# Top-k attention into a PReLU feed-forward: one Exp for two duos, scores copied two slots ahead, new slot orders, and the factor 1 - alpha moved from the output weights to the Relu

## The chip, the cores and the metric

The kernel runs on one core of a Trainium2 chip. The metric is the device time of one execution in microseconds. The core's engines each work through their own queue in order: TensorE (PE; its weight loads are shown as PEld), VectorE (DVE), ScalarE (ACT), GpSimd (POOL) and SyncE (SP, which here only issues DMAs).

## The reference

```python
# q, k, v: (8, 8, 576, 64); w_in (512, 2048); w_out (2048, 512); alpha (2048)
scores = q @ k.T / 8                                   # per batch and head
kth = np.partition(scores, -32, axis=-1)[..., -32:-31] # 32nd largest of each row
scores = np.where(scores >= kth, scores, -1e9)
attn = softmax(scores)
x = (attn @ v).transpose(0, 2, 1, 3).reshape(4608, 512)
h = x @ w_in
g = np.maximum(h, 0.0) + alpha * np.minimum(h, 0.0)
out = g @ w_out                                        # (4608, 512) float32
```

The kernel uses g = (1 - alpha) * relu(h) + alpha * h. The second term is linear in x, so w_in * alpha @ w_out is worked out once (tiles `w_lin_b`), and each output tile is the sum of x @ w_lin and of relu(h) with the factor 1 - alpha, times w_out.

## The kernel before

**Duos and slots.** The 8 x 8 x 576 score rows are cut into 144 "duos": two blocks of 128 query rows with 576 scores each (`duos`; 18 of a batch; "n" duos are the same rows of two heads, "m" duos collect the 64-row tails of heads). A software pipeline runs over slots n = 0 to 143, and a drain written out by hand follows. A duo d passes through these steps:

- `st_qk` (PE): scores into the one PSUM tile `ps_sc`, in slot d - 1; `st_exit` (ACT): one copy of 1,152 columns to an SBUF tile `s_sb`, at the end of slot d - 1. There are six `s_sb` tiles.
- the search, in slot d (DVE, in `dve_slot`): twelve MAX8 over groups of 96 scores into `up` and `small`. In odd slots the results of two duos go through `threshold_steps`: `fold` (two compares `bot` and `small`, four MAX8), `negate`, `least` (four MAX8) and `turn`, which writes the threshold into tile `p`.
- `st_count` in slot d + 2 (ACT): two Sign instructions with accumulator against that threshold into `sg`; `st_y` (POOL): two products `y`; `row` (DVE): one MAX8 over each `y`, into `p`.
- `pick_steps` (DVE) in even slots: three small instructions that give the exact 32nd value in `KZ`.
- `st_exp` (ACT) and `st_cut` (ACT, POOL) in slot d + 4: Exp of the duo's 1,152 scores into `w`, two Sign instructions against the exact threshold into `f`, the product `w` times `f` on POOL, then a DMA transpose (SP) to `wT`.
- `st_av` (PE) in slot d + 7 or d + 8, `norm_a` and `norm_b` (DVE) in even slots for two duos, then a DMA transpose to `xT`.

**Feed-forward.** When a chunk of `xT` is complete, `mlp_ready` queues hidden units (`h_pe`: matmuls into PSUM tile `ph`), Relus (`h_relu`, to `gT`) and output parts (`o_pe`: matmuls into `pz`; `o_act`: copy; `o_sp`: store). Slots take one or two of each; where nothing is ready `keep_warm` issues matmuls on the tile `idle`. `h_relu` is a DVE `tensor_scalar` with max, or on request an ACT Relu; the drain requests ACT ten times.

**Weights.** In slots 2 to 15 `w_out` comes as fp32 (`w_st`, POOL's queue), and `scale_out` makes two bf16 tiles of each of its 16 blocks: on ACT `w_out_b` = w_out * (1 - alpha), and on DVE `w_la` = w_out * alpha, of which the linear part is made.

**Order.** Every instruction goes through the class `Ordered`, so that each engine runs in the order of the program text; all of them therefore carry line 32 in the profile, and groups are told apart by tile names. The order inside a slot is the order of the statements in the loop `for n in range(ND)`. For ACT it is count, o_act, exp, cut, exit, copies of `qkT`; for DVE search, (fold,) Relu, (negate,) row 0, (least, turn,) norm, row 1, norm.

Of the kernel before, what the change touches and what calls it, by code (L numbers as in the profile page):

```python
# [17 lines left out]
NG = 6  # L18

# [40 lines left out]
def fast_path(tc, q, k, v, moe_w_in, moe_w_out, moe_alpha, out, flag):  # L60
# [16 lines left out]
    duos = []  # L77
# [15 lines left out]
    with ExitStack() as ctx:  # L93
# [5 lines left out]
        s_p = pool("s", 6)  # L99
# [47 lines left out]
        def sm(ins, reads, writes):  # L147
# [8 lines left out]
            DVE.small.add(ins.ins.name)  # L156
            recent.append((ins.ins, reads, writes))
            del recent[:-60]
# [10 lines left out]
        ws = [const.tile([128, 2, 640], BF16, name=f"w_{i}") for i in range(4)]  # L169
# [3 lines left out]
        alpha1m = const.tile([128, NFT], FP32, name="alpha1m")  # L173
        w_lin_b = [const.tile([128, DMODEL], BF16, name=f"w_lin_b{i}") for i in range(4)]
# [6 lines left out]
        for t in ws:  # L181
            POOL.memset(t[:, :, S:640], 0.0)
# [77 lines left out]
        def st_exit(n):  # L260
            s = s_p.tile([128, 2, S], FP32, name="s_sb", tag="s")
# [55 lines left out]
        def dve_slot(n, f_late):  # L317

            norm = norm_of(n)
            rows = duos_at("count", n)  # L320
# [15 lines left out]
            turn = None  # L336
            if n % 2:
                fold, negate, least, turn = threshold_steps(n // 2)
                fold()
                if n < ND - 1:  # L340
                    h_relu()
                negate()
            else:
                h_relu()
            for d in rows:
                row(d, 0)
            if turn:
                least()
                turn()
            if norm:  # L350
                norm_a(norm)
            for d in rows:
                row(d, 1)
            if norm:
                norm_b(norm)
            if f_late:
                h_pe()
                h_relu()
# [6 lines left out]
        for d in range(ND):  # L365
            for kind, lag in (("count", 2), ("cut", 4), ("exp", 4), ("av", 8 if d < 13 else 7)):
# [3 lines left out]
        for d in range(1, ND, 2):  # L370
            stage["norm", d + (8 if d < 13 else 7)] = d

        def st_count(n, rows=(0, 1)):
            s, p9 = T["s", n], T["p9", n // 2]
            if rows[0] == 0:
                T["sg", n] = two.tile([128, 2, S], BF16, name="sg", tag="sg", bufs=3)
                if n % 2 == 0:
                    T["cs", n // 2] = three.tile([128, 4], FP32, name="cs", tag="cs")
            sg, cs = T["sg", n], T["cs", n // 2]
            for i in rows:  # L380
                r = 2 * (n % 2) + i
                ACT.activation(sg[:, i, :], s[:, i, :], AF.Sign, bias=p9[:, r, 0:1], scale=-1.0,
                               accum_out=cs[:, r:r + 1])

        def st_y(n):
            y = two.tile([128, 2, S], FP32, name="y", tag="y")
            sg = T.pop(("sg", n))
            for i in range(2):
                POOL.tensor_tensor(y[:, i, :], T["s", n][:, i, :], sg[:, i, :], ALU.mult)
            T["y", n] = y  # L390
# [4 lines left out]
        def st_cut(n):  # L395
            w, s = ws[n % 4][:, :, 0:S], T.pop(("s", n))
            f = two.tile([128, 2, S], mybir.dt.uint8, name="f", tag="sg", bufs=3)
            for i in range(2):
                ACT.activation(f[:, i, :], s[:, i, :], AF.Sign, bias=KT[:, 2 * n + i:2 * n + i + 1])
            POOL.tensor_tensor(w, w, f.bitcast(mybir.dt.float8e4), ALU.mult)  # L400
# [162 lines left out]
        def h_relu(eng=None):  # L563
            if act:
                ch, f0, e_n, ph = act.pop(0)
                if eng is ACT:
                    ACT.activation(ch["g"][:, f0:f0 + e_n, :], ph, AF.Relu)
                else:
                    DVE.tensor_scalar(ch["g"][:, f0:f0 + e_n, :], ph, 0.0, None, ALU.max)
# [36 lines left out]
        for b in range(1, B):  # L606
            for i in range(KPB):
                p = KPB * b + i
                s0 = NB * (b - 1) + 4 + 4 * i + (2 if p == NPAIR - 2 else 0)
# [25 lines left out]

        def scale_out(f):
            if f % 8 == 0:
                hold["wl", f // 8] = gp.tile([128, 8, 512], BF16, name="w_la", tag="gT")
            src = hold["st", f // 4][:, f % 4, :]
            ACT.activation(w_out_b[f // 4][:, f % 4, :], src, AF.Copy, scale=alpha1m[:, f:f + 1])  # L640

            sm(DVE.tensor_tensor(hold["wl", f // 8][:, f % 8, :], src,
                                 alpha_ps[:, f:f + 1].to_broadcast([128, 512]), ALU.mult),
               [(304 + f, 305 + f)], [])
# [91 lines left out]
        for n in range(ND):  # L736
            now[0] = n
            run(n, "kd")
            o_sp()

            if n > 4 and not h_pe():
                keep_warm()
            wide_copy = n % 2 and (n, "prep") in todo
            if n > 3:
                run(n, "prep", 1)
            if n and on(n + 1):
                st_qk(n + 1)
            if n < 4:
                run(n, "prep", 2)
            if 0 < n < 5:  # L750
                keep_warm()
            for m in duos_at("av", n):
                st_av(m)
            late = len(hq) > (9 if n < 118 else 4 if n < 132 else 3) and n % 2 == 0 and not (on(n + 1) and duos[n + 1][0] == "m")

            for m in duos_at("count", n):
                st_count(m)
                st_y(m)
            if ready() > 4 or not wide_copy:
                o_act()  # L760
            for m in duos_at("exp", n):
                st_exp(m)
            if not norm_of(n):
                run(n, "ld")
            run(n, "lin_out")
            did = o_pe()
            run(n, "w")

            dve_slot(n, late)
            for m in duos_at("cut", n):  # L770
                st_cut(m)
            if n and on(n + 1):
                st_exit(n + 1)
            run(n, "cast")
            if (n, "lin") in todo:
                run(n, "lin")
            elif not ready() > (2 if n < 128 else 1) or on(n + 2) and duos[n + 2][0] == "m" or not o_pe():
                if n and not did:
                    keep_warm()
            while pend:  # L780
                short = len(pend[0][0].shape) == 3
                wide = pend[0][0].shape[1] == 512
                on_dve = n > 3 and (short and n > 16 or wide and (n < 17 or n % 2 == 0))
                prep_evac(DVE.tensor_copy if on_dve else ACT.copy)
            if n == 1:
                sm(DVE.tensor_copy(alpha_ps, aps), [], [(304, 320)])
                ACT.activation(alpha1m, aps, AF.Copy, scale=-1.0, bias=1.0)
            run(n, "scale")
            if norm_of(n):
                st_xT(norm_of(n) - 1)  # L790
                st_xT(norm_of(n))
                run(n, "ld")
# [42 lines left out]
        o_sp()  # L835
        st_av(D - 6)
        h_pe(2)
        h_relu(ACT)
        h_pe(2)
        h_relu(ACT)  # L840
        o_act()
        o_sp()
# [361 lines left out]
```

## Time and profile before

| | |
|---|---|
| median of 3 runs | 814.86 us (814.15 to 816.9) |
| profiled execution | 814.44 us, of which the span of the trace is 812.4 us |
| busy in the span | PE 734.3, DVE 755.8, ACT 767.0, POOL 713.6 us |
| mean granted TensorE clock | 0.994 |
| moved by DMA | 99.90 MB |

The span is the time from the first instruction to the last in the trace; 2.04 us of the profiled execution lie outside it. Busy time counts the union of an engine's instructions. On ACT and DVE the recorded instructions of one queue overlap at their ends, so the step from one start to the next is shorter than the recorded duration.

### The profile page before, as it was taken

How to read it: one execution, taken by the hardware profiler on the slowest of the kernel's cores; microseconds unless marked ns; L12 is line 12 of the kernel's file. 1: busy time of each engine (PE TensorE's matmuls, PEld its weight loads, DVE VectorE, ACT ScalarE, POOL GpSimd, SP SyncE). 2: the span in 40 equal slices, each digit the busy share in tenths (PEclk: the TensorE clock that was granted, in tenths of full speed). 3: DMA queues.
4: the chain of work that ended last, by engine and by line, in shares of the span. 5: the costliest groups of instructions: out<-in, count | busy, mean ns of one | idle time of the engine just before them, and what ended most of it. 6: DMA issues, size and time to landing. Idle time of an engine off the chain costs nothing.

```text
span 812.4 us, 17847 instructions
## 1 busy us (share of the span) xinstructions
PE 734.3 (90%) x5375; PEld 421.4 (52%) x5448; DVE 755.8 (93%) x3470; ACT 767.0 (94%) x1265; POOL 713.6 (88%) x565
## 2 busy tenths in 40 slices
PE   8888899989989998889989989898989999999886
PEld 5333455545545555555545555454545555556563
DVE  4999999999999999999999999999999999999961
ACT  5999999999999999999999999999999999999971
POOL 2898899999999999989999999999999988998860
PEclk9999999999999999999999999999999999999999
DMA  7799976665565575655576555665566565544361
GB/s 153 196 176 173 178 145 133 115 118 116 124 121 122 113 124 120 127 122 105 127 140 117 129 110 124 108 123 117 119 136 116 116 134 100 99 99 89 82 114 37
DMA packets 342327, 99.90 MB, mean 123 GB/s; under 512 B 336128, under 2 KB 336400, under 8 KB 342224
## 3 DMA queue, kind: packets, MB, share of 16 engines
q1 hardware_dynamic: 338928, 91.18, 58.0%
q0 software_dynamic: 1952, 7.09, 3.7%
q8 instruction: 45, 0.74, 0.4%
q10 hardware_dynamic: 1344, 0.43, 0.2%
q14 instruction: 58, 0.48, 0.2%
HBM read 36.71 MB, written 9.44 MB: 57 GB/s over the span
## 4 chain that ended last, share of the span: by engine, by line
DVE 33%; PE 22%; ACT 18%; POOL 12%; issue 10%; SPq 2%; DMA 2%; ACTq 0%; POOLq 0%; DVEq 0%
DVE small L32 11%; PE ps_sc L32 7%; DVE p L32 7%; POOL y L32 7%; DVE up L32 6%; PE pz L32 5%; ACT f L32 5%; ACT sg L32 4%; ACT s_sb L32 4%; POOL w L32 4%; PE ph L32 4%; DVE gT L32 4%; PE xo L32 3%; ACT w L32 3%; SPq L32 2%
## 5 line engine op out<-in xcount | busy, mean ns | idle before, releaser
L32 POOL TENSOR_TENSOR y<-s_sb,sg 128x576 f32<-128x576 f32 x288 | 362.2, 1279 | 25.2 <-ACT sg L32 24.5
L32 POOL TENSOR_TENSOR w<-w,f 128x1152 bf16<-128x1152 bf16 x142 | 317.8, 2238 | 45.8 <-ACT f L32 44.1
L32 ACT ACTIVATE sg<-s_sb,p 128x576 bf16<-128x576 f32 x288 | 221.6, 774 | 10.6 <-DVE p L32 8.3
L32 DVE MAX8 up<-s_sb 128x8 f32<-128x96 f32 x864 | 212.1, 245 | 11.0 <-ACT s_sb L32 10.9
L32 DVE MAX8 p<-y 128x8 f32<-128x576 f32 x288 | 215.0, 748 | 7.3 <-POOL y L32 6.4
L32 DVE MAX8 small<-s_sb 128x8 f32<-128x96 f32 x864 | 216.2, 250 | 0.0
L32 ACT ACTIVATE f<-s_sb,KZ 128x576 uint8<-128x576 f32 x284 | 203.8, 769 | 0.0
L32 PE MATMUL ps_sc<-qkT 64*128 64x512 f32 (+2 forms) x768 | 183.0, 566 | 22.9 <-ACT s_sb L32 22.5
L32 ACT ACTIVATE w<-s_sb 128x1152 bf16<-128x1152 f32 x144 | 166.9, 1159 | 0.0
L32 ACT COPY s_sb<-ps_sc 128x1152 f32<-128x1152 f32 x144 | 159.2, 1106 | 5.8 <-PE ps_sc L32 5.6
L32 PE MATMUL ph<-xT,w_in_b 128*128 128x256 bf16 (+1 forms) x1472 | 149.6, 249 | 7.0 <-DMA xT<-x 3.1
L32 PE MATMUL pz<-w_out_b,gT 128*128 128x512 bf16 x545 | 142.1, 379 | 9.4 <-issue 6.0
L32 PEld LDWEIGHTS <-w_in_b 128*128 128x128 bf16 x1472 | 119.6, 98 | 50.2 <-issue 10.0
L32 PE MATMUL xo<-v,wT 128*128 128x65 bf16 (+3 forms) x1600 | 126.1, 198 | 0.6 <-DVE x L32 0.6
L32 PEld LDWEIGHTS <-wT 128*128 128x128 bf16 (+3 forms) x1600 | 97.3, 99 | 28.9 <-issue 0.8
L32 DVE TENSOR_SCALAR gT<-ph 128x512 bf16<-128x512 f32 x134 | 90.4, 674 | 8.6 <-PE ph L32 8.6
L32 PEld LDWEIGHTS ps_sc<-qkT 64*128 64x128 f32 (+1 forms) x768 | 55.5, 169 | 66.8 <-ACT s_sb L32 35.0
L32 PEld LDWEIGHTS ps_sc<-kd,qkT 128*128 128x128 f32 x256 | 38.1, 188 | 97.1 <-issue 93.3
L32 PEld LDWEIGHTS <-gT 128*128 128x128 bf16 x576 | 54.6, 98 | 59.1 <-DVE gT L32 4.7
L32 PE MATMUL ps_sc<-kd,qkT 128*128 128x128 f32 x256 | 62.5, 326 | 0.0
L32 PE MATMUL rest<-idle 128*128 128x512 bf16 x200 | 52.5, 389 | 6.6 <-DVE gT L32 4.4
L32 ACT ACTIVATION_READ_ACCUMULATOR sg<-s_sb,p 128x1 f32 x288 | 56.2, 195 | 0.0
(67 smaller groups left out, 569.5 us busy)
## 6 DMA issues: line engine op xcount, KB each, us to landing
k_st<-in_k_dram SPq DMA_DIRECT2D x64, 128.0 KB, 2.8
v_st<-in_v_dram SPq DMA_DIRECT2D x64, 128.0 KB, 2.9
q_st<-in_q_dram SPq DMA_DIRECT2D x62, 128.0 KB, 2.7
out_dram<-o_sb SPq DMA_DIRECT2D x29, 256.0 KB, 2.5
w_st<-in_moe_w_out_dram POOLq DMA_DIRECT2D x4, 1024.0 KB, 7.3
wT<-w SPq DMA_TRANSPOSE x143, 3.5
w_in_b<-in_moe_w_in_dram POOLq DMA_DIRECT2D x4, 512.0 KB, 6.6
k_st<-in_k_dram SPq DMA_DIRECT2D x32, 32.0 KB, 2.6
```

Source lines behind the costliest of these rows:

```text
L32: ins = self.tc.keep_in_program_order(f(*a, **kw))
```

## The change

- One Exp instruction (`exp_two`) handles two duos (2,304 columns) from slot 17 on, at the end of every odd slot, behind the Signs. For that the six score tiles become one tile `s_all` and the four `w` tiles become two.
- From slot 8 on `st_qk` and `st_exit` work on duo n + 2 instead of n + 1.
- The statements of a slot become named steps, run in the order of a string; one string each for even and odd slots, before slot 18 and from it on. Each Sign and each half of `st_y` and `st_cut` has its own step. In odd slots the threshold steps `least` and `turn` come behind row 1, `fold` behind the Relu.
- The drain's order is a string too. All Relus are on DVE; the last pairs of Exps in the drain are two instead of four.
- `h_relu` computes max(h, 0) * (1 - alpha) with one `scalar_tensor_tensor`, whose second input is `alpha1m` broadcast along the tokens. `w_out_b` is loaded as bf16 by four DMAs on POOL's queue in slots 17, 19, 21 and 22; ACT's 16 products in `scale_out` go. DVE's 16 stay.
- Of the wide `qkT` copies of slots 4 to 17 those in odd slots go from DVE to ACT. The loads of `q` and of `v` are issued one slot later and one slot earlier, in most cases.

```diff
+LEAD = 8
+EV = "DADADADADADADADADA"
+SC = "DDDDDDDDDDDDDDDD"
+MODE = 18
+PAIRS = 18
+HEAD_E = "kd osp h prep qk av c0 c1 oact exp ld ope S R r0 na r1 nb late k0 k1 exit cast ope2 evac xt"
+HEAD_O = "kd osp h prep qk av c0 c1 oact exp ld ope S F R N r0 L T na r1 nb late E k0 k1 exit cast ope2 evac xt"
+EVEN = "kd osp h prep av c0 c1 oact ld qk ope S evac R r0 na r1 nb late k0 k1 exit cast ope2 xt"
+ODD = "kd osp h prep av qk ope c0 c1 oact ld S R F r0 N r1 L T late k0 k1 E evac exit cast ope2 xt"
+DRAIN = "osp a6 h RD h RD oact osp c1 p1 n6 RD c0 k3 r10 now op a5 op h op r11 RD h a4 r00 r01 k2 p0 n4 e1 RD oact osp h op e0 RD m1 m0 w2 op op oact osp h RD h RD tw a3 td h RD a1 a0 na nb h RD a2 n2 x0 ..."
...
+        wp = [const.tile([128, 4, 640], BF16, name=f"w_{i}") for i in range(2)]
+        ws = [wp[i // 2][:, 2 * (i % 2):2 * (i % 2) + 2, :] for i in range(4)]
+        s_all = const.tile([128, 12, S], FP32, name="s_sb")
...
         def st_exit(n):
-            s = s_p.tile([128, 2, S], FP32, name="s_sb", tag="s")
+            s = s_all[:, 2 * (n % 6):2 * (n % 6) + 2, :]
             ACT.copy(s, two_of(T.pop(("ps", n)), 960, S))
...
+        def exp_two(n):
+            c = 2 * (n % 6)
+            ACT.activation(wp[n // 2 % 2][:, :, 0:S], s_all[:, c:c + 4, :], AF.Exp, scale=att_scale)
...
-        def h_relu(eng=None):
+        def h_relu():
             if act:
                 ch, f0, e_n, ph = act.pop(0)
-                if eng is ACT:
-                    ACT.activation(ch["g"][:, f0:f0 + e_n, :], ph, AF.Relu)
-                else:
-                    DVE.tensor_scalar(ch["g"][:, f0:f0 + e_n, :], ph, 0.0, None, ALU.max)
+                DVE.scalar_tensor_tensor(out=ch["g"][:, f0:f0 + e_n, :], in0=ph, scalar=0.0,
+                                         in1=alpha1m[:, f0:f0 + e_n].unsqueeze(2).to_broadcast(list(ph.shape)),
+                                         op0=ALU.max, op1=ALU.mult)
...
-                at(s0 - 2, "ld", lambda p=p: load_one(p, "q"))
+                at(s0 - (2 if b == 1 else 1), "ld", lambda p=p: load_one(p, "q"))
-                at(s0 + 6 - early, "ld", lambda p=p: load_one(p, "v"))
+                at(s0 + (6 if b == 1 and i < 2 else 5) - early, "ld", lambda p=p: load_one(p, "v"))
...
+        def w_out_load(i):
+            POOL.dma_start(w_out_b[i], moe_w_out[512 * i:512 * i + 512, :].rearrange("(f p) n -> p f n", p=128))
...
-            ACT.activation(w_out_b[f // 4][:, f % 4, :], src, AF.Copy, scale=alpha1m[:, f:f + 1])
...
+            at((17, 19, 21, 22)[i], "w", lambda i=i: w_out_load(i))
...
+        def ahead(n):
+            return [m for m in ([n + 1] if n < LEAD else [n + 1, n + 2] if n == LEAD else [n + 2]) if n and on(m)]
...
+            def t_E():
+                if n % 2 and n >= PAIRS - 1 and on(n - 3):
+                    exp_two(n - 3)
```

In the strings S is the search, R the Relu, F, N, L, T are fold, negate, least and turn, r0 and r1 the rows, c0 and c1 a Sign of `st_count` with its `y`, k0 and k1 a Sign of `st_cut` (the product behind k1), na and nb the norm, evac the `qkT` copies; in the drain RD is a Relu, m a mask, e an Exp, a an `st_av`, and the digit counts back from the last duo.

More of the change, by code (lines that the diff above doesn't have):

```diff
@@ L734, in fast_path, with evac @@
         PE.transpose(aps, a16, ident_f[0:NFT, 0:NFT])
[L736 to L779, printed above, removed]
+        def ahead(n):
+            return [m for m in ([n + 1] if n < LEAD else [n + 1, n + 2] if n == LEAD else [n + 2]) if n and on(m)]
+        def evac(n):
             while pend:
@@ L794, in picked, with is_late @@
+        def is_late(n):
+            return len(hq) > (9 if n < 118 else 4 if n < 132 else 3) and n % 2 == 0 and not (on(n + 1) and duos[n + 1][0] == "m")
+        for n in range(ND):
+            slot(n)
         def picked(m):
```

316 lines of the change are left out of this document (175 added, 141 removed).

## The prediction

> **What bounds the kernel now.** First I cut the span into the stages by the table of busy time by window (window, its length, busy us of PE, PEld, DVE, ACT and POOL with instruction counts, clock, DMA share, GB/s).
>
> ```profile
> 0.00:20.00 20.00, 17.82 (x91) 11.45 (x92) 9.02 (x61) 11.69 (x24) 4.66 (x28) 1.00 0.73 155
> 20.00:120.00 100.00, 86.60 (x500) 40.97 (x502) 94.46 (x425) 98.43 (x168) 92.35 (x79) 0.97 0.93 176
> 120.00:760.00 640.00, 588.67 (x4358) 341.56 (x4422) 624.61 (x2897) 628.34 (x1028) 593.13 (x442) 1.00 0.59 118
> 760.00:812.40 52.40, 41.19 (x429) 27.46 (x436) 27.75 (x90) 28.51 (x49) 23.49 (x18) 0.97 0.39 74
> ```
>
> In the long middle stage ACT idles 11.7 us of 640 and DVE 15.4: two engines are full, POOL (46.9 idle) and PE (51.3) follow. In the weight stage (20 to 120) ACT alone is full (1.6 idle; DVE 5.5). In the drain none is. So a gain must take work or waiting off both ACT and DVE in the middle, off ACT in the weight stage. Next, what the idle time waits for, in the list of waits of the middle stage (us, times, longest), and the groups of POOL and of DVE's rows there:
>
> ```profile
> POOL w L32 <- ACT f L32: 39.0, 63, 1.1
> ACT sg L32 <- DVE p L32: 7.7, 20, 1.7
> DVE up L32 <- ACT s_sb L32: 5.5, 19, 0.4
> ACT s_sb L32 <- PE ps_sc L32: 1.5, 2, 1.3
> DVE p L32 <- POOL y L32: 1.4, 4, 0.4
> L32 POOL TENSOR_TENSOR y<-s_sb,sg 128x576 f32<-128x576 f32 x243 | 305.7, 1279 | 6.6 <-ACT sg L32 6.4
> L32 POOL TENSOR_TENSOR w<-w,f 128x1152 bf16<-128x1152 bf16 x121 | 270.9, 2239 | 40.3 <-ACT f L32 39.0 <-DVE p L32 1.0
> L32 POOL CAST v<-v_st 128x256 bf16<-128x256 f32 x52 | 20.8, 399 | 0.0
> L32 DVE MAX8 p<-y 128x8 f32<-128x576 f32 x242 | 180.8, 747 | 1.9 <-POOL y L32 1.4
> ```
>
> The two full engines wait for each other: DVE for the score copy (5.5), ACT for the threshold (7.7). 243 products y are 121.5 slots, so a slot takes 640 / 121.5 = 5.27 us and a pair of slots 10.53; the stage has 61 pairs.
>
> **One Exp for two duos.** Busy time misleads here, because ACT's records overlap. The timeline (start, duration) gives the true steps:
>
> ```profile
> 402.17 1.15 ACT L32 ACTIVATE w<-s_sb 128x1152 bf16<-128x1152 f32 x1
> 403.22 1.43 ACT L32 ACTIVATE f<-s_sb,KZ 128x576 uint8<-128x576 f32 x2
> 404.56 1.10 ACT L32 COPY s_sb<-ps_sc 128x1152 f32<-128x1152 f32 x1
> 405.55 0.78 ACT L32 ACTIVATE sg<-s_sb,p 128x576 bf16<-128x576 f32 x1
> ```
>
> An Exp occupies ACT for 403.22 - 402.17 = 1.05 us. No Exp of 2,304 columns is in the trace; I bound it by how ACT's time grows with columns:
>
> ```profile
> L32 ACT ACTIVATE f<-s_sb,KZ 128x576 uint8<-128x576 f32 x284 | 203.8, 769 | 0.0
> L32 ACT ACTIVATE w<-s_sb 128x1152 bf16<-128x1152 f32 x144 | 166.9, 1159 | 0.0
> L32 ACT COPY s_sb<-ps_sc 128x1152 f32<-128x1152 f32 x144 | 159.2, 1106 | 5.8 <-PE ps_sc L32 5.6
> L32 ACT COPY o_sb<-pz 128x512 f32<-128x512 f32 x35 | 19.8, 567 | 7.5 <-PE ph L32 6.3 <-PE pz L32 1.2
> ```
>
> From Sign to Exp it is (1159 - 769) / 576 = 0.68 ns a column, so 1,152 more columns cost 0.78 us and a pair saves 1.05 - 0.78 = 0.27. But the Sign reads a bias tile and the Exp does not; the two copies are of one kind and give (1106 - 567) / 640 = 0.84 ns, 0.97 us, and a saving of 0.08. No saving is the other end. I take 0.09: 61 x 0.09 = 5.5 us off ACT in the middle, ends 0 and 16.5. The Trainium skill (ScalarE: Activation LUTs, What ACT_TABLE_LOAD costs) says that each instruction with a tile as bias pays about 93 ns more and that neighbours overlap by as much; by it the wide Exp saves an estimated 93 ns a pair, against the 0.27 that the first reading of the rows offers.
>
> **Lead of two slots.** The copy that search n + 2 needs ends a whole slot, some 5 us, ahead, so the 5.5 us of DVE up <- ACT s_sb go. The qk matmuls still wait for the copy before, as now, in a PE with 51 us idle. The copy overwrites the tile of the duo whose Signs stand just ahead of it on ACT, and adds no wait. Next late for DVE is y.
>
> **New slot order.** DVE's timeline shows a stall inside its busy time:
>
> ```profile
> 407.30 0.24 DVE L32 MAX8 up<-s_sb 128x8 f32<-128x96 f32 x1
> 407.46 0.25 DVE L32 MAX8 small<-s_sb 128x8 f32<-128x96 f32 x1
> 407.74 0.25 DVE L32 TENSOR_TENSOR bot<-up,small 128x96 f32<-128x96 f32 x1
> ```
>
> Neighbouring MAX8 start 0.16 apart; bot starts 0.28 behind the one whose result it reads. With the Relu between them that 0.12 goes: 61 x 0.12 = 7.3 us. The threshold's last steps now stand behind row 1, so ACT's first Sign of an even slot gets it some 0.67 us later in DVE's order; that is priced among the rivals. Moving Exp behind the Signs of the cut lets POOL's product start a step of 1.05 earlier: part of its 39 us of waiting goes, on an engine that is not full.
>
> **Middle stage.** DVE sheds 5.5 + 7.3 = 12.8 us. ACT sheds 5.5 + 1.5 = 7.0 and can shed more only from its 7.7 us of waiting for the threshold, which arrives sooner when DVE no longer waits. The stage shrinks by something between 7.0 and 12.8; I take 10. Then ACT has 628.3 - 5.5 = 622.8 of 630, 98.9%, as full as now, which is why I don't take more. The ends are 0 (each wait is replaced by another) and 17 (ACT never idle).
>
> **The Relu with the factor.** The rows that bound its price:
>
> ```profile
> L32 DVE TENSOR_SCALAR gT<-ph 128x512 bf16<-128x512 f32 x134 | 90.4, 674 | 8.6 <-PE ph L32 8.6
> L32 DVE TENSOR_SCALAR neg<-small 128x128 f32<-128x128 f32 x72 | 20.2, 281 | 0.4
> L32 DVE TENSOR_TENSOR w_la<-w_st,small 128x512 bf16<-128x512 f32 x16 | 10.5, 675 | 0.0
> L32 DVE TENSOR_TENSOR small<-small,cs 128x36 f32<-128x36 f32 x72 | 13.3, 184 | 0.0
> L32 DVE SCALAR_TENSOR_TENSOR pk<-small,p 128x36 f32<-128x36 f32 x72 | 12.9, 179 | 0.1
> L32 DVE SCALAR_TENSOR_TENSOR w<-s_sb,KZ,w 128x576 bf16<-128x576 f32 x4 | 4.8, 1262 | 0.0
> L32 ACT ACTIVATE gT<-ph 128x512 bf16<-128x512 f32 x10 | 5.8, 593 | 7.1 <-PE ph L32 7.1
> ```
>
> The new form reads one input from PSUM (ph) and one from SBUF. The two-input w_la does so too, on as many columns, in 675 ns, one more than the Relu's 674; pk has the very operation, with operands placed alike, and takes no longer than the plain product of its size (179 to 184). The dear end is the mask, 1,262 for 576, but both its inputs are in SBUF; at its rate 512 columns are 1,122 ns. I take 675: nothing. The Trainium skill speaks against the change here: VectorE: DVE Perf Modes (The perf-mode tier table) grants an instruction with one tensor input up to twice the rate on PSUM, and one with two inputs never. It would cost if the old Relu ran at a doubled rate; by the rows it doesn't, (674 - 281) / 384 = 1.02 ns a column, hardly different from w_la's.
>
> **Weight stage.** ACT loses its products, DVE one wide copy.
>
> ```profile
> L32 ACT ACTIVATE w_out_b<-w_st,alpha1m 128x512 bf16<-128x512 f32 x16 | 11.4, 742 | 0.0
> 37.41 1.34 ACT L32 ACTIVATE w_out_b<-w_st,alpha1m 128x512 bf16<-128x512 f32 x2
> 38.65 0.77 ACT L32 ACTIVATE sg<-s_sb,p 128x576 bf16<-128x576 f32 x1
> w_st<-in_moe_w_out_dram POOLq DMA_DIRECT2D x4, 1024.0 KB, 7.3
> L32 POOL DMA_DIRECT2D w_st<-in_moe_w_out_dram x4 | 3.3, 818 | 0.0
> ```
>
> Two take 1.24 us, so 16 take 9.9. DVE, with 5.5 us idle, becomes the bound: I take 4 us, ends 0 and 5.5. The four bf16 loads cost POOL 4 x 0.82 = 3.3 us around slots 17 to 22, hidden by its idle time (about 0.4 us a slot, so several slots long), and land in 7.3 us, about a slot and a half; the output parts begin at slot 24. If that cover is gone it is 3.3 us. The q loads pass the DMA transposes of an even slot's end only to stand behind the next slot's short issues, in the place of v's, which moved the other way: nothing.
>
> **Drain.** Its chain runs over the masks:
>
> ```profile
> 771.03 1.06 ACT L32 ACTIVATE gT<-ph 128x512 bf16<-128x512 f32 x2
> 771.99 0.77 ACT L32 ACTIVATE sg<-s_sb,p 128x576 bf16<-128x576 f32 x1
> 773.64 4.99 POOL L32 TENSOR_TENSOR y<-s_sb,sg 128x576 f32<-128x576 f32 x4
> 781.01 4.82 DVE L32 SCALAR_TENSOR_TENSOR w<-s_sb,KZ,w 128x576 bf16<-128x576 f32 x4
> ```
>
> Two Relus (0.96 us of ACT) no longer stand ahead of the last Signs, but POOL starts the y's only at 773.64, 0.9 behind the end of the first Sign (771.99 + 0.77), so it is POOL that is late there and little is won. Two Relus now stand on DVE between the last rows and the masks: 2 x 0.67 = 1.35 us later. The other Relus find DVE idle (24.6 us of this stage), and the pair of Exps that left the drain costs nothing there. I take +0.7, ends -1 and +2.
>
> **The sum.** 812.4 - 10 - 4 + 0.7 = 799.1 us of span; with the 2.04 us outside it 801.1. The profiled execution (814.44) lies 0.42 under the median of the runs, so the median should be **801.5 us**.
>
> **The rivals.**
>
> *The waits change places.* The two engines stay as loosely full as now, because the threshold comes later in DVE's order and ACT's 7.7 us of waiting for it grow by what DVE stops losing. For it: both engines stand within 2.4% of full already. Against: the lead gives a slot of slack. The middle gains 0 to 3 us, the rest 4 - 0.7: 808.6 to 811.6.
>
> *The threshold loop becomes the bound (slower).* From one threshold to the next run a Sign (0.78), two y (2.56), the product (2.24), two y (2.56), row 1 and now least and turn behind it; with a row's MAX8 of 0.75 and two casts of 0.40 that is some 9.6 to 10 us of the pair's 10.53. It decides once it exceeds 10.5, and that needs only one o_sb copy of 0.57 ahead of the Sign. If each of the 35 falls on the loop, that is 35 x 0.57 = 20 us with no gain in the middle: 814.9 + 20 - 4 + 0.7 = 831.6. Against: today POOL waits 39 us for f, so this loop has slack, and f comes sooner.
>
> *The new Relu is dear (slower).* At the mask's rate it costs 1,122 - 674 = 0.45 us more, 57 us on some 128 Relus of the middle; DVE then needs 624.6 - 7.3 + 57.3 = 674.6 of it, 35 more than the stage lasts: 814.9 + 35 - 3.3 = 846.6. If instead the old Relu ran at double rate and the new one doesn't, half a nanosecond a column, 0.27 us, is added, and by the same working DVE needs 651.9: 823.5. That is the page's rule above; the slope of 1.02 ns speaks against it. It decides from about 0.1 us a Relu, where it eats the middle's gain.
>
> *The wide Exp saves nothing.* ACT's share falls from 7.0 to 1.5 us plus some waiting; the middle gains about 6: 805.5. It lies inside the forecast.
>
> **How the numbers follow.** The forecast with its ends (middle 6 to 17, weights 2 to 5.5, drain -1 to 2) covers 791 to 809 and has 0.62; 0.03 lies below it, where the fold's 7.3 us come on top. Waits that change places: 0.17, two thirds of it still faster by over 0.3% (2.4 us, about what a measurement of this kernel can tell from no change). The loop 0.10, the dear Relu 0.05 (0.02 of it by the rule), a late weight load or drain 0.03, slower by a few us. So faster 0.62 + 0.03 + 0.11 = 0.76, same 0.06, slower 0.18. The range 790 to 815 leaves out 0.03 below and 0.17 above.
>
> **What would show it.** Right: Exps of 128x2304 at about 2.1 us in the groups; gT as a two-input instruction near 675 ns; no line DVE up <- ACT s_sb; ACT idle in the middle about as now, the middle some 10 us shorter; ACT below DVE in the weight stage, 4 us shorter. Wrong: ACT sg <- DVE p well over 8 us (waits changed places), POOL y <- ACT sg and DVE p <- POOL y grown together (the loop), or gT above 780 ns.

## The result and the profile after

The changed kernel takes 821.95 us in the median (821.65 to 823.64, 4 runs), the kernel before 814.73 beside it: 1.0084 times as long [1.0061, 1.0106]. The profiled execution took 821.81 us, its span 820.0. Forecast were 801.5 us; the range ended at 815.

The page of the changed kernel (all instructions carry line 42 there; the last row is of its DMA issues, with KB each and us to landing):

```profile
PE 730.9 (89%) x5367; PEld 423.4 (52%) x5440; DVE 754.4 (92%) x3479; ACT 752.3 (92%) x1177; POOL 716.8 (87%) x567
DVE  4989966999999999999999999999999899999972
L42 POOL TENSOR_TENSOR y<-s_sb,sg 128x576 f32<-128x576 f32 x288 | 362.7, 1281 | 67.8 <-ACT sg L42 67.8
L42 DVE MAX8 p<-y 128x8 f32<-128x576 f32 x288 | 215.6, 750 | 28.1 <-POOL y L42 26.9
L42 ACT ACTIVATE w<-s_sb 128x2304 bf16<-128x2304 f32 (+1 forms) x80 | 153.6, 1920 | 15.9 <-DMA wT<-w 15.9
L42 DVE SCALAR_TENSOR_TENSOR gT<-ph,alpha1m 128x512 bf16<-128x512 f32 x144 | 97.4, 677 | 11.2 <-PE ph L42 11.2
w_out_b<-in_moe_w_out_dram POOLq DMA_DIRECT2D x4, 512.0 KB, 6.6
```

ACT's busy time fell from 767.0 to 752.3 us, and the time did not follow. DVE's row of 40 slices (a digit is the busy share in tenths) has a hole of two sixes after some 100 us that was not there, and a wait is new: the Exps wait 15.9 us in all for DMA transposes of `w`. The table of busy time by window (columns as in the prediction) shows the hole; first the kernel before, then the changed one:

```profile
100.00:150.00 50.00, 48.94 (x333) 26.80 (x337) 47.32 (x229) 49.86 (x84) 47.08 (x37) 1.00 0.69 131
200.00:600.00 400.00, 363.09 (x2630) 209.16 (x2667) 391.88 (x1826) 394.75 (x646) 372.90 (x280) 1.00 0.61 122
```

```profile
100.00:150.00 50.00, 39.67 (x244) 20.74 (x246) 35.14 (x168) 38.96 (x58) 37.89 (x32) 0.90 0.98 154
200.00:600.00 400.00, 360.80 (x2651) 211.26 (x2688) 391.75 (x1842) 396.20 (x612) 376.26 (x282) 1.00 0.61 122
```

Between 100 and 150 us DVE does 12.2 us less work and ACT 10.9 less, while the DMA share goes from 0.69 to 0.98. The granted clock of TensorE falls to 0.90 there; in e5 below it is 0.93 in the same window, and e5 loses nothing in slots 20 to 23, so a lower clock alone doesn't cost the time. From 200 to 600 both engines are as full as before.

To place the difference I read the start of each slot's first search (MAX8 into `up`) from both traces. The "lag" is how far the changed kernel is behind the one before at that slot (at slot 0 it is -0.3; in most runs below it lies within 0.4 of zero there, in e13 at +1.9):

| at slot | 18 | 20 | 24 | 118 | 119 | 143 | end |
|---|---|---|---|---|---|---|---|
| lag, us | -0.9 | +3.6 | +11.2 | +7.3 | +10.0 | +8.1 | +7.7 |

So the stage up to slot 18 gave 0.9 us, slots 18 to 23 lost 12.1, slots 24 to 117 won back 4.0, slot 118 lost 2.7, the slots after it won 1.9 and the drain 0.4. In the undisturbed slots 40 to 112 a pair takes 10.406 us instead of 10.512. Three questions follow: what happens in slots 18 to 23, what in slot 118, and why a pair wins 0.11 us instead of 0.16.

ACT's timeline of the changed kernel through the hole (start, duration, in brackets the idle time and its releaser), then POOL's and SP's (issues of DMAs):

```profile
104.82 2.12 ACT L42 ACTIVATE w<-s_sb 128x2304 bf16<-128x2304 f32 x1 [3.38 <-DMA wT<-w]
135.36 2.12 ACT L42 ACTIVATE w<-s_sb 128x2304 bf16<-128x2304 f32 x1 [7.30 <-DMA wT<-w]
139.34 1.28 POOL L42 TENSOR_TENSOR y<-s_sb,sg 128x576 f32<-128x576 f32 x1 [6.79 <-ACT sg L42]
102.79 0.82 POOL L42 DMA_DIRECT2D w_out_b<-in_moe_w_out_dram  x1
118.86 3.80 SPq L42 DMA_TRANSPOSE wT<-w  x1
122.76 3.13 SPq L42 DMA_TRANSPOSE w_inT<-w_in_b  x1
125.98 1.18 SPq L42 DMA_DIRECT2D kd<-qkT  x2
127.22 1.90 SPq L42 DMA_DIRECT2D k_st<-in_k_dram  x3
129.23 5.54 SPq L42 DMA_TRANSPOSE wT<-w  x2
```

The wide Exp overwrites the `w` of the two duos before the last pair, so their transposes must have read it. For the wait of 7.30 us, the transposes that SP issues at 118.9 and 129.2 are late, because SP's issues themselves got long: a transpose of `w` takes SP 1.35 us in the median, here 3.80, and between two of them stand a weight transpose (3.13) and the DMAs of `kd` and `k_st`. The Signs of the next duo stand behind the Exp on ACT, POOL waits 6.8 us for them and DVE for POOL. The wait of 3.38 us is another case: its transposes were issued at 97.1 and 100.0 us, before the first load of `w_out_b` at 102.8, and e5 below waits as long without that load. The view of DMA issues, 100 to 145 us of the kernel before and then 96 to 142 of the changed one (count, KB, us to landing):

```profile
xT<-x SPq DMA_TRANSPOSE x2, 2.5
k_st<-in_k_dram SPq DMA_DIRECT2D x4, 128.0 KB, 3.1
```

```profile
q0 software_dynamic: 1584, 1.57, 25.8%
xT<-x SPq DMA_TRANSPOSE x2, 7.4
k_st<-in_k_dram SPq DMA_DIRECT2D x2, 128.0 KB, 6.2
w_out_b<-in_moe_w_out_dram POOLq DMA_DIRECT2D x4, 512.0 KB, 6.6
```

While the four loads of `w_out_b` run (POOL's software queue, q0, takes a quarter of the DMA engines' time there), two transposes of `xT` take three times as long and two loads of `k` twice as long. Not all are slowed so much: the median of `wT` goes from 3.5 to 3.8 us, that of `q` stays at 2.7.

### The profile page after: what moved, and what is told of

It reads as the page before. It is cut to its first block, busy times and chain, and to the rows that moved or that the text cites. A ratio compares the mean times of both kernels' runs of the same rounds, so it can differ in the third digit from the quotient of the medians.

```text
span 820.0 us, 17771 instructions
## 1 busy us (share of the span) xinstructions
PE 730.9 (89%) x5367; PEld 423.4 (52%) x5440; DVE 754.4 (92%) x3479; ACT 752.3 (92%) x1177; POOL 716.8 (87%) x567
## 4 chain that ended last, share of the span: by engine, by line
DVE 37%; ACT 18%; POOL 16%; issue 12%; PE 12%; DMA 3%; SPq 0%; ACTq 0%; POOLq 0%; DVEq 0%
DVE small L42 11%; DVE p L42 11%; POOL y L42 11%; ACT sg L42 8%; DVE up L42 6%; ACT f L42 5%; DVE gT L42 4%; POOL w L42 4%; ACT s_sb L42 3%; PE pz L42 3%; PE ps_sc L42 3%; PE ph L42 3%; DMA wT<-w 2%; PE xo L42 2%; DVE x L42 1%
## 5 line engine op out<-in xcount | busy, mean ns | idle before, releaser
L42 ACT COPY s_sb<-ps_sc 128x1152 f32<-128x1152 f32 x144 | 160.4, 1114 | 12.3 <-PE ps_sc L42 10.2
L42 ACT ACTIVATE w<-s_sb 128x2304 bf16<-128x2304 f32 (+1 forms) x80 | 153.6, 1920 | 15.9 <-DMA wT<-w 15.9
L42 PEld LDWEIGHTS <-wT 128*128 128x128 bf16 (+3 forms) x1600 | 94.5, 99 | 54.5 <-issue 19.7
L42 DVE SCALAR_TENSOR_TENSOR gT<-ph,alpha1m 128x512 bf16<-128x512 f32 x144 | 97.4, 677 | 11.2 <-PE ph L42 11.2
L42 PE MATMUL rest<-idle 128*128 128x512 bf16 x192 | 50.0, 388 | 3.5 <-DVE gT L42 1.4
```

Of the source, the lines that this page charges most:

```text
L42: ins = self.tc.keep_in_program_order(f(*a, **kw))
```

## The experiments

All are edits of the changed kernel unless another is named. Times are medians; the ratio is to the kernel before, run on the same chip.

**Slots 18 to 23: the loads or the wide Exp.** Three kernels. `e2_wout_on_act`: `w_out` scaled on ACT as before, the plain Relu, no loads.

```diff
-                DVE.scalar_tensor_tensor(out=ch["g"][:, f0:f0 + e_n, :], in0=ph, scalar=0.0, ...)
+                DVE.tensor_scalar(ch["g"][:, f0:f0 + e_n, :], ph, 0.0, None, ALU.max)
+            ACT.activation(w_out_b[f // 4][:, f % 4, :], src, AF.Copy, scale=alpha1m[:, f:f + 1])
-            at((17, 19, 21, 22)[i], "w", lambda i=i: w_out_load(i))
```

> The changed kernel with w_out scaled on ACT and the plain Relu as before; no w_out loads in slots 17 to 22; the Relu stays on DVE. Theory 2 (the loads hold up the transposes): the stalls of 3.4 and 7.3 us go and the time falls by 8 to 11 us, less up to 4 us for ACT's 16 products in the weight stage: 812 to 817. Theory 1 (the wide Exp alone): the w_in transposes and the loads of k, q and v are still there, the stalls stay for the most part, 819 to 824. gT at 674 instead of 677 ns makes 0.4 us either way.

`e3_single_exp`: one Exp for each duo, in every slot behind the Signs of `st_count` (the drain's string alike).

```diff
-PAIRS = 18
+PAIRS = 200
-EVEN = "... c0 c1 oact ld ..."
+EVEN = "... c0 c1 oact exp ld ..."
-ODD = "... c0 c1 oact ld ..."
+ODD = "... c0 c1 oact exp ld ..."
```

> The changed kernel with one Exp for each duo in its old place (ahead of the Signs of the cut), four slots of slack against the transposes. Theory 1: all 15.9 us of ACT's waiting for the transposes go, and ACT pays 0.09 us a pair, 5.5 us, back, half of it seen: 810 to 815. Theory 2: 818 to 823, the lateness shows at the matmuls that read wT. Theory 3: f comes later and POOL's product with it, 822 or more.

`e5_loads_early`: the four loads in slots 0, 1, 1 and 3.

```diff
-            at((17, 19, 21, 22)[i], "w", lambda i=i: w_out_load(i))
+            at((0, 1, 1, 3)[i], "w", lambda i=i: w_out_load(i))
```

> The changed kernel with the four w_out loads in slots 0, 1, 1 and 3 instead of 17, 19, 21 and 22. Theory 2 (the loads, on top of the transposes and the loads of q, k and v, jam the DMA queues in slots 18 to 24): the 12 us lost there shrink to 1 to 3, as in the kernel with w_out on ACT, and up to 4 us are lost in slots 0 to 8, where the weights already come in: 811 to 815. Theory 1 (the wide Exp's two slots of slack are enough to lose it): 819 to 823.

| kernel | time, us | ratio | lost in slots 18, 19 | lost in slots 20 to 23 |
|---|---|---|---|---|
| changed: wide Exp, loads there | 821.95 | 1.0084 [1.0061, 1.0106] | 4.5 | 7.6 |
| e3: narrow Exps, loads there | 838.86 | 1.0291 [1.0262, 1.032] | 0.6 | 7.3 |
| e5: wide Exp, loads earlier | 823.34 | 1.0095 [1.0075, 1.0116] | 4.0 | 0.0 |
| e2: wide Exp, no loads | 819.48 | 1.0046 [1.0033, 1.006] | 0.8 | -0.3 |

The loads cost 7.3 to 7.6 us in slots 20 to 23 with either Exp, and nothing is lost there without them. Only the way differs. With narrow Exps ACT does not wait for a transpose, but PE waits for `k` and for `wT`; PE's timeline of e3:

```profile
132.18 0.63 PE L42 MATMUL tps<-ident_f,k_st 128*128 128x128 f32 x4 [2.64 <-DMA k_st<-in_k_dram]
133.34 1.06 PE L42 MATMUL xo<-v,wT 128*128 128x65 bf16 x10 [0.54 <-DMA wT<-w]
```

The loss of 4 us in slots 18 and 19 takes the wide Exp: it stays when the loads leave (e5) and goes when the Exps are narrow (e3). It also depends on when ACT gets there. In the changed kernel, in e5 and in e2 the first wide Exp starts within 0.1 us of the landing of the last transpose that it needs (at 104.73, 115.59 and 109.38 us). In e2 ACT, which has its products again, gets to it only 0.6 us before that landing, so it hardly waits, and 0.8 us are lost. ACT's timeline of e5, then of e2:

```profile
115.67 2.12 ACT L42 ACTIVATE w<-s_sb 128x2304 bf16<-128x2304 f32 x1 [3.45 <-DMA wT<-w]
109.46 2.12 ACT L42 ACTIVATE w<-s_sb 128x2304 bf16<-128x2304 f32 x1 [0.57 <-DMA wT<-w]
```

None of the three is a faster kernel, though. e5 lost 10.5 us in slot 0, where the loads stood ahead of the first `q` (PE's list of waits below), e2 reaches slot 18 7.4 us later than the changed kernel, since the 16 products are back on ACT, and e3 lost 0.34 us in every pair.

```profile
PE tps L42 <- DMA q_st<-in_q_dram: 17.6, 10, 9.0
```

**Slot 118.** In the changed kernel SP issues the last batch's loads of `v` and of `q` in one slot, ahead of three transposes, and PE waits for `q`:

```profile
630.31 1.86 SPq L42 DMA_DIRECT2D v_st<-in_v_dram  x3
632.22 1.83 SPq L42 DMA_DIRECT2D q_st<-in_q_dram  x3
634.16 6.98 SPq L42 DMA_TRANSPOSE wT<-w  x3
635.81 0.63 PE L42 MATMUL tps<-ident_f,q_st 128*128 128x128 f32 x4 [2.70 <-DMA q_st<-in_q_dram]
```

`e9_v_last_batch` moves that `v` back to its slot of before; `e7_qv_loads_old` moves nearly all loads of `q` and `v` back.

```diff
-                at(s0 + (6 if b == 1 and i < 2 else 5) - early, "ld", lambda p=p: load_one(p, "v"))
+                at(s0 + (6 if b == 1 and i < 2 or b == B - 1 else 5) - early, "ld", lambda p=p: load_one(p, "v"))
```

> The changed kernel with v of the last batch loaded one slot later, where it was before, so that in slot 115 SP issues q ahead of nothing but the transposes; all else as changed. If slot 118 loses its 3.2 us because v and q stand in one slot ahead of the transposes that the wide Exp waits for: slot 118 at 5.3 to 5.7 us instead of 8.5, the time 818 to 819.5. If not: 821 to 823.

> The changed kernel with the loads of q and v in the slots of the kernel before. If their new slots cause the 3.2 us that slot 118 loses (PE waits 2.7 us for q there, then ACT 2.7 for the transposes): 3 us faster, 818 to 820. If the loss at 118 comes from the preparation of the last pair but one, a slot earlier: within 1.5 us of 822. If the old places stand against the new order of SP's queue: 823 to 827.

In e9 slot 118 lasts 5.71 us instead of 8.49 (before: 5.78), and PE's wait is 0.47:

```profile
630.46 1.86 SPq L42 DMA_DIRECT2D q_st<-in_q_dram  x3
632.42 4.58 SPq L42 DMA_TRANSPOSE wT<-w  x2
637.06 1.84 SPq L42 DMA_DIRECT2D v_st<-in_v_dram  x3
633.72 0.63 PE L42 MATMUL tps<-ident_f,q_st 128*128 128x128 f32 x4 [0.47 <-DMA q_st<-in_q_dram]
```

The cause of slot 118 is shown. The medians don't show these 2.8 us: e9 took 821.18 us, 1.0088 [1.0063, 1.0113], where the changed kernel has 1.0084, and its four runs spread from 819.2 to 826.3. e7 took 828.11 us, 1.0166 [1.0141, 1.019]: slot 118 is mended there too, but other slots get long (8.3 us in slot 108), a pair takes 0.27 us more, and the wide Exp waits 21.8 us for transposes instead of 15.9. So the old places of the loads don't suit the changed order.

**Why a pair wins only 0.11 us.** `e4_lead_one` takes the second slot of lead away:

```diff
-LEAD = 8
+LEAD = 200
```

> The changed kernel with the scores copied one slot ahead throughout. If the lead of two slots is worth what DVE no longer waits for the copy (5.5 us in the middle before): 825 to 829. If PE or ACT pays for the lead, or the wait was hidden behind others: 818 to 822. The slots 18 to 24 should lose 11 to 12 us in either case.

ACT's timeline of the changed kernel, then of e4, an even slot each:

```profile
403.01 1.45 ACT L42 ACTIVATE f<-s_sb,KZ 128x576 uint8<-128x576 f32 x2
404.49 1.12 ACT L42 COPY s_sb<-ps_sc 128x1152 f32<-128x1152 f32 x1
408.37 2.11 ACT L42 ACTIVATE w<-s_sb 128x2304 bf16<-128x2304 f32 x1
410.38 1.10 ACT L42 COPY s_sb<-ps_sc 128x1152 f32<-128x1152 f32 x1
```

```profile
404.19 1.45 ACT L42 ACTIVATE f<-s_sb,KZ 128x576 uint8<-128x576 f32 x2
405.53 1.11 ACT L42 COPY s_sb<-ps_sc 128x1152 f32<-128x1152 f32 x1
```

With two slots of lead the copy starts 1.48 us behind the two Signs' start, with one 1.34, as in the kernel before (403.22 to 404.56 in the prediction's lines). Over slots 40 to 112 the step from the second Sign to the copy is 800 ns in the median against 666. With two slots of lead the copy goes into the tile that these Signs read, and starts only behind their end, where neighbours otherwise overlap. The wide Exp occupies 2.01 us (408.37 to 410.38) where two narrow ones take 2 x 1.054: it saves 94 ns a pair, and the copy gives 134 ns back. Still the lead pays: e4 takes 827.87 us, 1.0142 [1.0091, 1.0193], a pair 0.24 us more, and DVE waits 35.9 us for the score copy instead of 3.9.

`e6_copy_covered` puts, in even slots, the copies of an output part (`oact`) and of `qkT` on ACT between the Signs and the score copy, and in odd slots the `qkT` copy on DVE; `e8_old_order` goes back to the order of before on PE and DVE (fold right behind the search, least and turn ahead of row 1). The strings that show it, of e6 the even one, then of e8 the odd one:

```diff
-EVEN = "kd osp h prep av c0 c1 oact ld qk ope S evac R r0 na r1 nb late k0 k1 exit cast ope2 xt"
+EVEN = "kd osp h prep av c0 c1 ld qk ope S R r0 na r1 nb late k0 k1 oact evac exit cast ope2 xt"
```

```diff
-ODD = "kd osp h prep av qk ope c0 c1 oact ld S R F r0 N r1 L T late k0 k1 E evac exit cast ope2 xt"
+ODD = "kd osp h prep qk av c0 c1 oact ld ope S F R N r0 L T na r1 nb late k0 k1 E exit cast ope2 evac xt"
```

> The changed kernel with another order in the steady slots: in even slots the o_sb copy and the qkT copy stand on ACT between the cut's Signs and the score copy, in odd slots the qkT copy goes to DVE. Theory 4 (with a lead of two slots the copy overwrites the tile that the Signs just ahead of it read, and waits 0.134 us for their end in every even slot, which eats the 0.096 us a pair that the wide Exp saves): where another instruction stands between, in three of four even slots, the 0.134 go; ACT sheds some 6 us, and the time falls by 3 to 6 us to 816 to 819. Theory 5 (the steady slots are bound by DVE or by the threshold's way through POOL, not by ACT): no change within 1.5 us, or slower by the copies' new places.

> The changed kernel with the steady slots' statements in the order of before on PE and DVE (search, fold, Relu, negate, row 0, least, turn, row 1; qk ahead of av; the qkT copies last); on ACT the wide Exp stays behind the Signs of the cut. If the new order is worth the fold's stall of 0.12 us a pair and a little more: 5 to 10 us slower, 827 to 832. If ACT is the bound and DVE's stall was hidden: 820 to 824. If the threshold's later place cost time: faster, 815 to 820.

e6 (833.85 us, 1.0211 [1.0177, 1.0244]) took the 134 ns away where another copy stood between, yet its pair takes 10.607 us. ACT's timeline shows the output copy and the score copy 0.47 us apart, without the wait; but elsewhere the score copy now waits for PE's scores, 8 times and 5.7 us in all from 200 to 600 us (the `qkT` copies moved too; whether that is why is not shown). So that the 134 ns set the length of a pair is worked out, not shown: no run took them away and nothing else.

```profile
410.99 0.57 ACT L42 COPY o_sb<-pz 128x512 f32<-128x512 f32 x1
411.46 1.11 ACT L42 COPY s_sb<-ps_sc 128x1152 f32<-128x1152 f32 x1
401.24 1.12 ACT L42 COPY s_sb<-ps_sc 128x1152 f32<-128x1152 f32 x1 [0.97 <-PE ps_sc L42]
```

e8 (834.4 us, 1.0236 [1.0195, 1.0278]) needs 10.538 us a pair, 0.13 more than the changed kernel, all of it in odd slots: the new order is worth about what the fold's stall was priced at. With the Relu ahead of it `bot` starts in the changed kernel 0.59 us behind the Relu, whose own length is 0.68, so the stall is gone; DVE's timeline:

```profile
407.44 0.68 DVE L42 SCALAR_TENSOR_TENSOR gT<-ph,alpha1m 128x512 bf16<-128x512 f32 x1
408.03 0.24 DVE L42 TENSOR_TENSOR bot<-up,small 128x96 f32<-128x96 f32 x1
```

**Is the threshold loop near?** `e1_exp_later` puts the wide Exp behind the Signs of `st_count` of the next even slot, so that it has a slot's time more for its transposes but stands ahead of the Signs for `f` (the drain's string alike).

```diff
-EVEN = "... c0 c1 oact ld ..."
+EVEN = "... c0 c1 oact E ld ..."
-ODD = "... k0 k1 E evac ..."
+ODD = "... k0 k1 evac ..."
-                if n % 2 and n >= PAIRS - 1 and on(n - 3):
-                    exp_two(n - 3)
+                if n % 2 == 0 and n >= PAIRS:
+                    exp_two(n - 4)
```

> The changed kernel with the wide Exp moved from the end of an odd slot to the next even slot, behind its two Signs of the count: some 2 to 3 us more until it overwrites the w tiles that SP's transposes still read. Theory 1 (the wide Exp, which has two slots of slack against the transposes where the narrow Exps had four, stalls ACT for 15.9 us, and that is what cost the slots 18 to 24): the stalls shrink to under 8 us in total and the time falls by 6 to 10 us from 822, to 812 to 816. Theory 2 (the four w_out loads hold up the DMA queues and the stage would be late whatever waits): the stall moves to the transposes' other reader, and the time stays at 819 to 823. Theory 3 (the step from threshold to threshold over ACT and POOL is the bound): the even slots, where the threshold is awaited, get longer, 825 or more.

e1 takes 894.26 us, 1.0973 [1.0948, 1.0997]. A pair takes 11.64 us, and the list of waits of e1 goes round in a ring that POOL, DVE and ACT close:

```profile
POOL w L42 <- ACT f L42: 109.8, 68, 2.1
DVE p L42 <- POOL y L42: 81.0, 130, 1.9
ACT sg L42 <- DVE p L42: 69.1, 61, 3.4
```

Here the loop of the prediction's second rival is the bound. The `f` of even slots stand 2.0 us later in ACT's order and a pair grew by 1.23, so in the changed kernel the loop has an estimated 0.8 us of slack. There it isn't the bound: from 200 to 600 us ACT never waits for the threshold. What POOL and DVE wait for there in the changed kernel:

```profile
POOL y L42 <- ACT sg L42: 23.1, 37, 1.5
DVE p L42 <- POOL y L42: 6.4, 18, 0.9
```

In the kernel before POOL waits 24.4 us for `f` and 2.5 for `sg` in that window, so it idles no more than before. DVE idles as much as before (8.1 us, now 8.3): the 3.6 us for the score copy are gone, but its waits for `y` grew from 0.8 to 6.4.

**Versions that keep the gain and avoid the loss.** `e12_no_loads`: as e2, and the wide `qkT` copies on DVE, the second slot of lead from slot 20, the wide Exp from slot 19 on with narrow ones behind `oact` until then, and the `v` of e9. `e13_with_loads` is e12 with the loads and the new Relu. `e14` and `e15` are e12 with the lead from slot 16 and from slot 8; `e16` is e15 with the `qkT` copies alternating again. `e10` and `e11` put the new order and the wide Exp off to slot 24 (e11 without the loads).

The settings of e12, an excerpt; the rest is as in e2 and e9:

```diff
-LEAD = 8
-EV = "DADADADADADADADADA"
-PAIRS = 18
+LEAD = 20
+EV = "DDDDDDDDDDDDDDDDDA"
+PAIRS = 20
```

> w_out scaled on ACT and the plain Relu on DVE as before, no w_out loads; copies of slots 4 to 17 and the lead as before until slot 20, wide Exp from slot 19, but the steady orders from slot 18 as in the change (the kernel with both halves kept the old orders until slot 24, and so put q's loads of slots 19 to 23 behind an odd slot's transposes); v of the last batch one slot later. If the steady part's 0.1 us a pair is a gain of its own and the loads cause what slots 18 to 24 lose: at most 3 us behind at slot 24, 2 to 4 us ahead at slot 114, 809 to 813. If slots 18 to 24 lose 8 us or more here too, the loss belongs to the step into the new orders and not to the loads: 817 to 821.

> The same kernel with the factor at the Relu and the four w_out loads in slots 17 to 22, so that the two differ in this part alone. If the loads jam the queue that the transposes stand in: 8 to 12 us behind the kernel without loads at slot 24 (a little less for ACT's 16 products that are gone from the weight stage), 816 to 822. If only the wide Exp's early start in slot 17 was at fault: within 2 us of it.

> The kernel without w_out loads, with the lead of two slots from slot 16 instead of 20. In slot 20 PE issued the scores of two duos, waited 2.8 us for the first to be copied, and the hidden units behind them came 4.9 us late for the Relu: slot 21 lasted 10.3 us instead of 5.4. In slot 16 no Relu waits yet. If that step is what is left of the loss: at most 2 us behind the kernel before at slot 24, 2 to 3 us ahead at the end, 811 to 813, faster than both kernels. If the double copy costs as much wherever it stands: 814 to 816.

> As e12_no_loads, but with the second slot of lead taken in slot 8 again, as in the changed kernel, where the one slot with two score computations cost 1.6 us instead of some 5 in slot 20. If the double copy is what slot 21 of e12 paid for: slots 18 to 24 lose under 2 us, the steady gain of 0.06 to 0.1 us a pair stays, and the time is 811 to 814 us, below both kernels. If the loss at slot 20 comes from the change of order and of the Exp there, not from the lead: 815 to 819 us.

> As e15, and the wide copies of qkT of slots 4 to 17 alternate between DVE and ACT, as in the changed kernel. With the products of w_out kept on ACT this loads ACT in the weight stage: 1 to 4 us slower than e15 by slot 18 if ACT is the bound there, the same as e15 within 1 us if the threshold loop is.

> The changed kernel with the new slot orders and the wide Exp from slot 24 on instead of 18, so that the stage with the w_out loads runs with narrow Exps, four slots of slack and the old order. If the wide Exp's short slack is what turns late transposes into a stall there (about 4 of the 12 us that slots 18 to 24 lose, after the 7.9 of the kernel with narrow Exps throughout): 816 to 819, the slots 18 and 22 at 5 to 7 us instead of 9.3 and 11.6. If the loads alone cost the 12 us: 820 to 823.

> The parts of the change that gained, without those that lost: w_out scaled on ACT and the plain Relu on DVE as before, no w_out loads; up to slot 17 the copies and the lead as before (lead of two from slot 20); new orders and wide Exp from slot 24; v of the last batch one slot later. From the slots of the runs so far: no loss up to slot 24 beyond 1 to 2 us for the second copy and the first wide Exp, then 0.1 us a pair, 5 to 6 us, gained up to slot 114, nothing lost at 118: 809 to 812, faster than before by 3 to 6 us. If the steady gain came only from catching up on what slots 18 to 24 had lost: 814 to 817.

| kernel | time, us | ratio | lag at slot 18 | at 24 | at 143 |
|---|---|---|---|---|---|
| e12 | 815.16 | 1.0 [0.9988, 1.0011] | 0.3 | 6.0 | 1.2 |
| e13 | 820.79 | 1.0075 [1.0056, 1.0094] | 1.5 | 10.0 | 6.2 |
| e14 | 819.79 | 1.0053 [1.0036, 1.007] | 9.1 | 10.1 | 6.1 |
| e15 | 816.28 | 1.0016 [0.9995, 1.0037] | 3.4 | 5.2 | 1.4 |
| e16 | 815.73 | 1.0009 [1.0, 1.0018] | 6.2 | 7.4 | 3.0 |
| e10 | 830.59 | 1.0187 [1.0173, 1.0201] | -1.5 | 14.5 | 13.9 |
| e11 | 821.35 | 1.0091 [1.0067, 1.0114] | -0.4 | 11.3 | 8.3 |

e12 against e13 prices the loads with the new Relu, less ACT's products, at 5.6 us; from slot 17 to 24 e13 loses 5.2 us more than e12. e12 and e14 show another cost: the one slot in which PE works out two duos' scores into the single `ps_sc`, which ACT must empty in between, cost 5 us at slot 20 and 9 at slot 16. PE's timeline of e12 there:

```profile
123.07 2.08 PE L42 MATMUL ps_sc<-qkT 64*128 64x512 f32 x4 [2.79 <-ACT s_sb L42]
```

In slot 8 it costs 3 us (slot 9 lasts 9.41 us in e15, 6.56 in e12), and e15 then loses only 1.8 us from 18 to 24. But what is saved there is paid before: e15 ends level with the kernel before, as e12 does, and so does e16, though its alternating copies cost 2.8 us more by slot 18. e10 and e11 tell nothing about the loads: slot 23 lasted 15.5 us in e10 and 12.3 in e11, which has no loads. By the text of the program the old order, held until slot 24, puts the `q` loads of those slots behind the transposes of odd slots; no run tests whether that is why. No version beat the kernel before.

## Why the prediction was wrong

Forecast were 13.3 us less span; it grew by 7.7 us, the lag at the end. Of that 12.1 were lost in slots 18 to 23 and 2.7 in slot 118; 0.9, 5.8 and 0.4 were won up to slot 18, in the other slots behind 24 and in the drain.

**Loads of w_out: the step that failed most.** The prediction priced them on POOL's queue and by their landing time, 3.3 us at worst. It did not ask what shares the DMA engines with them, though its own first fence showed the DMA share at 0.93 in the weight stage. They cost 7.3 to 7.6 us in slots 20 to 23, as the first table of the experiments shows. The trace of before had a sign of it: SP's longest issue of a transpose of `w`, 4.84 us against 1.35 in the median, falls into a load of `w_st` on POOL's queue (issued at 42.04, landed 8.07 us later):

```profile
45.16 4.84 SPq L32 DMA_TRANSPOSE wT<-w  x1
```

That the transfers slow one another is what the issues and the landing times say; through which resource is not shown.

**The overwriting of w: a missing step.** The wide Exp writes two duos' `w` at once into one of two tiles, and so needs transposes that were issued two slots ago, where each narrow one had four tiles to go round. The prediction priced the instruction's length and put this wait at nothing; it is 15.9 us in the whole trace, and the loss of some 4 us in slots 18 and 19 depends on it (e3 against e5). A third tile pair would test it alone; that wasn't tried.

**"Adds no wait": wrong.** The copy two slots ahead waits 134 ns an even slot for the Signs that read its tile (e4). By length this takes back more than the wide Exp's 94 ns. The price of the wide Exp itself was right: 0.09 us taken, 0.094 measured. It was the estimate that the Trainium skill (ScalarE: Activation LUTs, What ACT_TABLE_LOAD costs) gives, too, and the trace agrees with it.

**Middle stage, 10 us: mis-sized.** From slot 24 to 143 5.8 us were won outside slot 118. The fold's stall went (odd slots 5.43 to 5.29 us) and DVE's waits for the score copy went, as forecast; even slots grew from 5.08 to 5.12. Two losses stand against the gain: the 134 ns, and row 1 in even slots, which starts 238 ns behind the reciprocal instead of 81, since it waits for `y` (82 in e8, which has the old order). The prediction named the threshold's later place but counted its price among the rivals only, not in the sum. The changed kernel's 10.41 us a pair is also the best of its kind: ten other kernels with the same steady order lie between 10.44 and 10.48, a gain of 0.03 to 0.07 us, so the second digit of these prices is not settled.

**q and v loads: "nothing" was wrong.** It cost 2.7 us in slot 118 (e9), where the two shifts met in one slot; with the old places a pair takes 0.27 us more (e7).

**Weight stage, 4 us: too much.** It gave 0.9, or 0.6 counted from slot 0. Up to the start of slot 17 the change gave 1.6 us, and e4, which takes no second slot of lead, 3.6: the products were worth nearly what was forecast there, but the second copy in slot 8, which the prediction didn't price, took 2 us back. With the products on ACT that step costs 3.1 us by slot 18 (e15 against e12) and the `qkT` copies 2.8 (e16 against e15). Then slot 17, where the kernel before needs 5.38 us, takes 6.39 in the changed kernel and 8.63 in e4, with the first wide Exp's wait in it, and 7.75 in e13, which has narrow Exps there and where DVE waits 2.28 us for PE's `xo`. So the gain is mostly given back at the step into the new order, not by one cause.

**Right:** the new Relu costs nothing, 677 ns against 674, so the rate of up to double that the Trainium skill (VectorE: DVE Perf Modes, The perf-mode tier table) allows a one-input instruction on PSUM was not there to lose. The dear end of that price was misread: the mask's 1,262 ns are the mean of one mask of 2,635 and three of 805 (last section), so at the mask's undisturbed rate 512 columns are an estimated 716 ns. The drain was within 1.1 us (-0.4 against +0.7), but partly by luck: its first mask took 0.84 us instead of 2.63, which the prediction didn't count.

**The rivals.** None happened as described. Of the first one, waits that change places, a part did: DVE lost its waits for the score copy and got waits for `y` in their place, though ACT's wait for the threshold went. The threshold loop didn't bind, but e1 shows how near it is; the terms that the prediction lists for it add up to 10.4 us rather than 9.6 to 10, and the slack from e1 makes it an estimated 9.6. The first sign given for it (`y` and `p` waiting longer) appeared without it: POOL's idle time only changed its label.

## What to carry to other kernels

A load on another queue can still slow the transfers that the chain waits for: look at the DMA share of the stage where it lands, at how long transfers there take beside other loads, and at the oldest transfer that an instruction waits for. When buffers or instructions are merged, price the write as well as the work: ask what read the target last, and how many slots ago. A change that gains 0.1 us a slot pair can be outweighed by one bad slot, so list the slots where the old and the new order meet before summing the steady state.

## What the runs showed of the hardware

An ACT instruction that overwrites a tile that the one before it reads starts 134 ns later than one that doesn't (800 against 666 ns behind a Sign). A DMA transpose of `w` occupies SP's issue for 1.35 us in the median and for 3.8 and 4.1 while loads of `w_out_b` run; one of `w_in_b` took 6.06 then. The mask, a DVE instruction with both inputs in SBUF, took 2,635 ns in the kernel before when it started 0.2 us behind POOL's last product, which ran 2.2 us; the three masks behind it took 805 each. In the changed kernel the first started 0.2 us before that product ended and took 835, the others 806. In both kernels the first mask ends 0.6 us behind the product's end. That the product held it up fits these times; no run tests it. The tile's view (shortest, median, longest in ns), before and after:

```profile
L32 DVE SCALAR_TENSOR_TENSOR w<-s_sb,KZ,w x4: 805/805/2635, 781.0 to 785.0; 128x576 bf16<-128x576 f32 x4
L42 DVE SCALAR_TENSOR_TENSOR w<-s_sb,KZ,w x4: 806/806/835, 790.7 to 792.9; 128x576 bf16<-128x576 f32 x4
```
